# Where the first image's value rows are loaded and cast, and who copies the bias table: an attention and snake-MLP kernel on Trainium2

## The chip, the cores and the metric

The kernel runs on one NeuronCore of one Trainium2 chip. The metric is the device time of one execution in microseconds (us). The kernel before was timed in three runs: 383.49, 385.6 and 383.82 us, median 383.82. Its profile is of one more execution, of 383.39 us.

The engines of the core run independently and meet at semaphores: PE (matrix products), DVE (elementwise, reads PSUM), ACT (activation functions, reads PSUM), POOL (elementwise on SBUF, and the issuer of the software DMA queue q0, the only one here that casts while it copies) and SP (only issues DMAs, on the hardware queue q1). ACT can issue DMAs too (queue q10). Each engine does its own instructions strictly in the order in which the program emits them.

## The reference

```python
def _attn_ref(q, k, v, bias_table):            # (8, 8, 576, 64) each; table (32, 8)
    scores = scale * np.matmul(q, k.transpose(0, 1, 3, 2))
    ...                                        # bucket[i, j] depends on |i - j| only
    scores = scores + bias_table[bucket].transpose(2, 0, 1)[None]
    attn = np.exp(scores - np.max(scores, axis=-1, keepdims=True))
    attn = attn / (np.sum(attn, axis=-1, keepdims=True) + 1e-09)
    return np.matmul(attn, v)

def _moe_ref(x, w_in, w_out, alpha):           # x: (4608, 512), w_in (512, 2048)
    h = x @ w_in
    s = np.sin(alpha * h)
    return (h + s * s / (alpha + 1e-09)) @ w_out
```

There are 8 images of 8 heads. Each has 576 positions of 64 numbers. The bias of a pair of positions depends on their distance alone and is constant beyond 128 positions. The attention result of an image, heads side by side, is the input of the MLP.

## The kernel before, in words

**Per image t (0 to 7).** Heads are taken in pairs p = 0..3, and the pairs in groups g = 0, 1. A score unit is a pair of matmuls (two heads) into two PSUM banks: kind "A" is 128 keys by 512 queries for two heads, kind "C" the last 64 keys, kind "B" the last 64 queries (`plan_unit`, L638). ACT exponentiates a unit (L672) into the tile `u`. The bias enters afterwards as a product: DVE multiplies the band near the diagonal by exp(bias), tiles `m2r` and `mhr` (L696 and L681). The products with the values (`plan_av`, L830) take `v` and `vh` (values with a column of ones, so that the row sums come along); DVE normalizes (L864, L865), and the result is transposed into `xT` (on PE with a copy by ACT or DVE for image 0, by DMA later). In image 0 a group has ten units, eight "A" and two "C"; its "B" units are done later, among image 1 (`plan_late`).

**MLP per block b of 512 tokens.** `plan_moe_in` (L905): 16 tiles f of h = w_in^T x, 4 matmuls each; ACT sine (L929); a square by ACT or DVE; DVE forms g (L943). `plan_mo` (L975): 64 matmuls g^T w_out, used by the planner to fill PE while ACT exponentiates.

**The order.** A planner (class `Plan`, L60 to L196) decides at build time. Each task has a cost per engine, dependences, a priority and an earliest time `nb`; `run` simulates the engines and emits tasks in the order of that simulation. The constants `T_...` (L207 to L225) are such earliest times in us. They set only the order: on the chip an instruction starts when its engine has reached it and its semaphores allow it. A DMA issue also waits until the DMA issued eight places earlier on the same kind of queue (q0; SP and ACT together) has landed, since there are eight completion semaphores for each.

**The start, image 0.** Written out by hand from L480 to L533, then by the planner.

- k and q of pair 0 come in 32 bits on SP (L486, L487) and are cast by DVE, ACT and POOL (L519 to L523). Pairs 1 to 3 come by cast loads on POOL (`load_pair`, L492, L606). PE transposes each (`plan_tr`, L560: six transposes for pair 0, twelve for the others), and kT and qT are copied out of PSUM by DVE, or ACT for qT of pair 0 (`T_ACT`). POOL makes a block-diagonal copy of the last keys, `kt` (L598).
- The bias: ACT issues the loads of the table and of a constant `phi` (L488, L489), PE multiplies (L515), ACT exponentiates (`tabE`, L516), PE spreads it with `phi` (L518), DVE copies the result to `e_sb` (L520), ACT writes it to `e_dram` (L528), and SP reads it back in skewed windows as `m2r` and `mhr` (L529 to L532).
- The values: SP loads all of image 0 in 32 bits into a part of the tile of `w_out`: heads 0 to 3 and the last 64 rows early (L507 to L509), heads 4 to 7 behind the band rows (L533). POOL casts them to `v` and `vh` (L526, L419) in a fixed chain of nine tasks in `plan_v0`, and the products of group 0 and 1 depend on them (`vdone`, L856).
- alpha: SP loads `alphaN` and an identity `idf` (L510, L511), PE transposes (L626), DVE forms `alphaT` and `inv_a` (L629 to L633). The earliest time is 8.6 (`T_AL`).
- Image 1's values are loaded in 32 bits into `v1st` and cast by POOL (`loads3`, L540). POOL clears image 1's `kt`, `vh`, `v` (`clear`, L497) at the start. `load_w_in16` (L428), k and q of image 1 (`nat2`, L537) and `load_w_out16` (L434) follow on POOL, `w_in` in two halves.
- `warm` (L453) is matmuls on zeros.

Of the kernel before, what the change touches and what calls it, by code (L numbers as in the profile page):

```python
# [10 lines left out]
F16 = mybir.dt.float16  # L11
# [44 lines left out]
class Cell:  # L56
    v = None
# [150 lines left out]
T_WI = 15.0  # L208
T_FIRST = (4.9, 5.8)
T_PAIR = ((7.0, 7.4), (10.4, 11.0), (12.4, 13.0))  # L210
T_ACT = (0,)
T_M2 = (12.0, 13.5, 14.5, 14.5)
T_MH = 13.0
T_V0 = (8.0, 8.8, 9.6, 10.4, 11.0, 14.2, 14.8, 15.4, 16.0)
T_AL = (8.6, 100)
LATE = 100
T_LD = 27.0
# [4 lines left out]
T_V = (0.0, 50.0)  # L222
T_TR1 = (35.0, 36.5)
T_W = (22.5, 28.0)
T_WO = (40.0, 43.0, 46.0, 49.0)  # L225
WARM0 = 5
WARM1 = 1
# [20 lines left out]
def kernel(  # L248
# [45 lines left out]
    idf = nc.inline_tensor(np.eye(NF, dtype=np.float32), "identf")  # L294
# [15 lines left out]
    wv = w_out16.rearrange("p f n -> p (f n)")  # L310
    v1st = sgl.tile([128, 2 * (4 * H + NP) * D], F16, name="v1st")
    vst, vhst = [], []
    for x in (wv, v1st):
        n4 = 2 * 4 * H * D
        y = x[:, 0:n4].bitcast(F32)
        vst.append(y.rearrange("p (c h d) -> p c h d", c=4, h=H) if vst else
                   y.rearrange("p (y h c d) -> p y h c d", y=2, c=4, h=H // 2))
        vhst.append(
            x[:, n4 : n4 + 2 * NP * D].bitcast(F32).rearrange("p (hp d) -> p hp d", hp=NP)
        )  # L320
# [72 lines left out]
    def load_v16(t):  # L393
        vp = v[t].rearrange("h s d -> s h d")
        for c in range(4):
            nc.gpsimd.dma_start(  # L396
                out=vs[t % 2][:, c, :, 0:D], in_=vp[128 * c : 128 * c + 128],
            )
        vq = v[t].rearrange("(hp two) s d -> two s hp d", two=2)
        for z in range(2):  # L400
            nc.gpsimd.dma_start(
                out=vhs[t % 2][64 * z : 64 * z + 64, :, VC * z : VC * z + D], in_=vq[z, 512:S]
            )

    def load_v32(t, eng):
        vp = v[t].rearrange("h s d -> s h d")
        for c in range(4):
            eng.dma_start(out=vst[t][:, c], in_=vp[128 * c : 128 * c + 128])
        vq = v[t].rearrange("(hp two) s d -> two s hp d", two=2)
        for z in range(2):  # L410
            eng.dma_start(out=vhst[t][64 * z : 64 * z + 64], in_=vq[z, 512:S])

    def cast_v(t, eng, cs):
        for c in cs:
            if c < 4:
                eng.tensor_copy(out=vs[t][:, c, :, 0:D], in_=vst[t][:, c])
                continue
            z = c - 4
            eng.tensor_copy(  # L419
                out=vhs[t][64 * z : 64 * z + 64, :, VC * z : VC * z + D],  # L420
                in_=vhst[t][64 * z : 64 * z + 64],
            )
# [30 lines left out]
    def warm(n, k=7):  # L453
        for _ in range(n):
            full(pb[:, k, :], zz[:, 0:128], zz, True, True)
# [41 lines left out]
    clear(P_, 1)  # L497
    vp = v[0].rearrange("h s d -> s h d")
    vq = v[0].rearrange("(hp two) s d -> two s hp d", two=2)

    def v0_in(y, eng):
        for h in range(4):
            eng.dma_start(
                out=vst[0][:, y, h], in_=v[0, 4 * y + h, 0:512].rearrange("(c p) d -> p c d", p=128)
            )

    v0_in(0, nc.sync)  # L507
    for z in range(2):
        nc.sync.dma_start(out=vhst[0][64 * z : 64 * z + 64], in_=vq[z, 512:S])  # L509
    nc.sync.dma_start(out=alphaN, in_=moe_alpha.rearrange("(f p) -> f p", p=128))  # L510
    nc.sync.dma_start(out=idf_sb, in_=idf.ap())  # L511
# [5 lines left out]
    warm(WARM1)  # L517
    full(pb[0:H, 0, 0:EW], tabE, phi_sb, True, True)  # L518
    cast0(0, nc.vector)  # L519
    nc.vector.tensor_copy(out=e_sb, in_=pb[0:H, 0, 0:EW])  # L520
# [3 lines left out]

    def cast_v0(h):
        P_.tensor_copy(out=vs[0][:, :, h, 0:D], in_=vst[0][:, h // 4, h % 4])  # L526

    nc.scalar.dma_start(out=e_dram.ap(), in_=e_sb)  # L528
    load_m2r(nc.sync, 0, 2)  # L529
    load_mhr(nc.sync)  # L530
    load_m2r(nc.sync, 2, 4)
    load_m2r(nc.sync, 4, H)  # L532
    v0_in(1, nc.sync)  # L533
# [6 lines left out]
    def loads3():  # L540
        load_v32(1, P_)
        stage_kq(2)
        cast_v(1, P_, range(6))
# [59 lines left out]

    def plan_v0():
        for p in range(2, NP):
            plan.add({"POOL": 1.5}, lambda e, p=p: load_pair(p), [], -950 + 200 * (p - 2), nb=5.8)  # L606
        for i in range(9):
            vdone.append(plan.add(
                {"POOL": 0.7 if i == 4 else 0.4},
                lambda e, i=i: cast_v(0, P_, (4, 5)) if i == 4 else cast_v0(i if i < 4 else i - 1), [],  # L610
                9000 + i, nb=T_V0[i], after=vdone[-1:]))

        def rest(e):
            load_w_in16(1, (0, 2))
            loads2()

        x = plan.add({"POOL": 1.2}, lambda e: load_w_in16(0, (0, 2)), [], -400, nb=T_WI)
        x = plan.add({"POOL": 6.0}, rest, [], 9006, nb=T_WI + 3.0, after=vdone[-1:] + [x])
        plan.add({"POOL": 8.0}, lambda e: loads3(), [], 9007, nb=T_LD, after=[x])

# [462 lines left out]
```

## Time and profile before

| | before |
|---|---|
| three runs, median | 383.82 us (383.49 to 385.6) |
| the profiled execution | 383.39 us, of which the span of instructions is 381.6 |
| PE busy | 368.8 us (97%) |
| ACT busy | 313.9 us (82%) |
| DVE busy | 270.0 us (71%) |
| POOL busy | 92.5 us (24%) |
| share of the chain that ended last: PE, DMA | 86%, 8% |
| queue q0 (POOL): packets, MB | 90112, 18.06 |
| queue q1 (SP): packets, MB | 53520, 22.24 |
| first exponential of image 0 starts, last one ends | 9.26, 29.22 |
| first matmul on w_in, on w_out | 31.11, 48.86 |

A line of a timeline has the start, the duration, the engine, the line of the kernel, the operation, the tiles written and read, the count, and in brackets the idle time of the engine before it with what ended that. A line of the view by stretches has the stretch, and for PE, PE's weight loads, DVE, ACT and POOL the busy time and count, then the granted PE clock, the DMA engines' share and GB/s.

### The profile page before, as it was taken

The numbers are of one execution on the slowest core, as the hardware profiler recorded it, in microseconds if no ns is written. First come the engines' busy times: TensorE is split into PE (matmuls) and PEld (weight loads), VectorE is DVE, ScalarE is ACT, GpSimd is POOL, SyncE is SP. The second block draws the span as 40 slices with busy tenths as digits, with TensorE's granted clock in tenths as the row PEclk, the third lists the DMA queues.
The fourth block names the chain that finished last, engine by engine and source line by source line (L and its number), as shares of the span: only waits on it lengthen the run. The fifth ranks groups of instructions, "written<-read, shape, count | busy, mean of one in ns | idle before, by whom it ended". The sixth has DMA issues, their size and how long they took to land.

```text
span 381.6 us, 8918 instructions
## 1 busy us (share of the span) xinstructions
PE 368.8 (97%) x3545; PEld 200.5 (53%) x3545; DVE 270.0 (71%) x601; ACT 313.9 (82%) x432; POOL 92.5 (24%) x130
## 2 busy tenths in 40 slices
PE   6789999999999999999999999999999999999995
PEld 3355445644465446784564456544677456444442
DVE  4596997679676967697768867796769676999000
ACT  2798999879996999699988999699969997998111
POOL 7385371055000630046001900082005000000000
PEclk9999999999999999999999999999999999999999
DMA  9889999299713997279927991599239512000212
GB/s 179 163 153 206 198 214 161 60 165 123 81 48 86 159 132 90 78 137 115 137 52 155 94 161 51 112 117 155 56 92 141 59 53 78 3 0 3 82 55 82
DMA packets 143785, 40.90 MB, mean 107 GB/s; under 512 B 131624, under 2 KB 137824, under 8 KB 143744
## 3 DMA queue, kind: packets, MB, share of 16 engines
q0 software_dynamic: 90112, 18.06, 55.5%
q1 hardware_dynamic: 53520, 22.24, 24.3%
q8 instruction: 27, 0.44, 0.5%
q14 instruction: 14, 0.11, 0.1%
q10 hardware_dynamic: 112, 0.05, 0.1%
HBM read 37.73 MB, written 16.52 MB: 142 GB/s over the span
## 4 chain that ended last, share of the span: by engine, by line
PE 86%; DMA 8%; POOL 2%; ACT 2%; SPq 1%; DVE 0%; issue 0%; ACTq 0%; DVEq 0%
PE pb L451 85%; DMA nat<-in_q_dram 4%; DMA w_out<-in_v_dram 1%; DMA e_dram<-e_sb 1%; DMA xT<-xn 1%; DMA phi_sb<-phi_const 1%; POOL w_in L432 1%; PE pb L889 1%; ACT u L672 1%; PE pb L575 0%; POOL v L526 0%; SPq L467 0%; ACT kT L556 0%; SPq L474 0%; ACT s L929 0%
## 5 line engine op out<-in xcount | busy, mean ns | idle before, releaser
L672 ACT ACTIVATE u<-pb 128x1024 f16<-128x1024 f32 (+1 forms) x174 | 152.5, 963 | 11.4 <-PE pb L451 10.3
L451 PE MATMUL pb<-w_out,g 128*128 128x512 f16 x576 | 139.0, 380 | 0.1
L451 PE MATMUL pb<-xT,w_in 128*128 128x512 f16 (+4 forms) x704 | 128.0, 340 | 0.1
L929 ACT ACTIVATE s<-pb,alphaT 128x512 f16<-128x512 f32 x144 | 93.0, 687 | 14.8 <-PE pb L451 14.6
L943 DVE SCALAR_TENSOR_TENSOR g<-sq,inv_a,pb 128x512 f16<-128x512 f16 x144 | 101.1, 743 | 3.5 <-ACT sq L936 2.1
L451 PEld LDWEIGHTS <-w_in 128*128 128x128 f16 x704 | 64.1, 98 | 56.0 <-issue 0.6
L696 DVE TENSOR_TENSOR u<-u,m2r 128x512 f16<-128x512 f16 (+1 forms) x128 | 63.4, 504 | 30.8 <-ACT u L672 29.8
L451 PEld LDWEIGHTS <-g 128*128 128x128 f16 x576 | 52.9, 98 | 60.4 <-issue 8.5
L451 PEld LDWEIGHTS <-u 128*128 128x128 f16 x1404 | 53.6, 97 | 11.0 <-issue 3.8
L451 PE MATMUL pb<-v,u 128*128 128x65 f16 x1248 | 53.5, 193 | 0.0
L391 POOL COPY kt<-kT 64x256 f16<-64x256 f16 x12 | 5.4, 447 | 178.2 <-DMA kT<-staged_k 142.3
L451 PE MATMUL pb<-qT,kT 64*128 64x64 f16 (+1 forms) x512 | 43.6, 290 | 1.4 <-ACT u L672 0.9
L938 DVE TENSOR_TENSOR sq<-s 128x512 f16<-128x512 f16 x80 | 34.1, 431 | 10.9 <-ACT s L929 10.0
L936 ACT ACTIVATE sq<-s 128x512 f16<-128x512 f16 x64 | 40.4, 634 | 0.9
L451 PE MATMUL pb<-vh,u 128*128 128x130 f16 x156 | 34.4, 220 | 0.1
L865 DVE TENSOR_TENSOR xn<-pb,rd 128x256 f16<-128x256 f32 (+1 forms) x64 | 30.9, 482 | 2.4 <-DVE rd L864 0.2
L556 ACT ACTIVATE outs<-pb 128x512 f32<-128x512 f32 x15 | 9.0, 598 | 28.1 <-PE pb L451 28.1
L451 PEld LDWEIGHTS <-kT 64*128 64x128 f16 x512 | 16.8, 94 | 24.1 <-issue 16.4
L396 POOL DMA_DIRECT2D v<-in_v_dram x24 | 21.2, 898 | 0.1
L864 DVE RECIPROCAL rd<-pb 128x4 f32<-128x4 f32 (+1 forms) x64 | 11.9, 186 | 11.1 <-PE pb L451 10.0
L1004 ACT ACT_TABLE_LOAD x15 | 19.2, 1283 | 0.3
L558 DVE COPY outs<-pb 128x512 f32<-128x512 f32 x21 | 14.5, 689 | 4.0 <-PE pb L451 4.0
(80 smaller groups left out, 165.5 us busy)
## 6 DMA issues: line engine op xcount, KB each, us to landing
out_dram<-outs SPq DMA_DIRECT2D x36, 256.0 KB, 2.1
staged_k<-in_k_dram POOLq DMA_DIRECT2D x6, 576.0 KB, 8.2
staged_q<-in_q_dram POOLq DMA_DIRECT2D x6, 576.0 KB, 10.9
v<-in_v_dram POOLq DMA_DIRECT2D x24, 128.0 KB, 4.8
w_in<-in_moe_w_in_dram POOLq DMA_DIRECT2D x4, 512.0 KB, 7.6
w_out<-in_moe_w_out_dram POOLq DMA_DIRECT2D x4, 512.0 KB, 18.9
w_out<-in_v_dram SPq DMA_DIRECT2D x8, 128.0 KB, 6.2
v1st<-in_v_dram POOLq DMA_DIRECT2D x4, 256.0 KB, 18.1
```

The source lines that it names most:

```text
L396: nc.gpsimd.dma_start(out=vs[t % 2][:, c, :, 0:D], in_=vp[128 * c : 128 * c + 128],)
L451: nc.tensor.matmul(out=out, lhsT=lhsT, rhs=rhs, start=start, stop=stop)
L558: k_of(e).tensor_copy(out=o, in_=i)
L672: nc.scalar.activation(out=o, in_=x, func=AF.Exp, scale=0.125)
L696: nc.vector.tensor_tensor(out=io, in0=io, in1=m2[:, 2 * p : 2 * p + 2, x0 : x0 + hi - lo], op=ALU.mult)
L864: nc.vector.reciprocal(out=r, in_=x[:, :, :, D])
L865: nc.vector.tensor_tensor(out=xn.v[:, 0:nq].rearrange("p c (z d) -> p c z d", z=2), in0=x[:, :, :, 0:D], in1=r.unsqueeze(3).to_broadcast([ ...
L929: nc.scalar.activation(out=s16.v, in_=h.v, func=AF.Sin, scale=alphaT[:, f : f + 1])
L936: nc.scalar.activation(out=sq.v, in_=s16.v, func=AF.Square)
L938: k_of(e).tensor_tensor(out=sq.v, in0=s16.v, in1=s16.v, op=ALU.mult)
L943: nc.vector.scalar_tensor_tensor(out=gcell[b].v[:, f, :], in0=sq.v, scalar=inv_a[:, f : f + 1], in1=h.v, op0=ALU.mult, op1=ALU.add,)
L1004: nc.scalar.preload_act_table_set(name)
```

## The change

1. **Values of image 0.** Heads 0 to 3 and the last 64 rows are cast loads on POOL's queue (six DMAs, tasks of `plan_v0`); heads 4 to 7 still come in 32 bits on SP, behind the band rows, and four POOL copies cast them. The early loads of SP go. The products of group 0 no longer carry a planned dependence on `vdone`; they have the earliest times 17 and 19 (`T_V`).
2. **Bias table.** The copy to `e_sb` moves from DVE to ACT, and it and its matmul become planned tasks (`plan_table`); the matmul falls between the six k and the six q transposes of pair 0.
3. **Copies.** `T_ACT` is empty: DVE also copies qT of pair 0.
4. **alpha.** `alphaN` is loaded behind the values on SP; the identity is a POOL copy of a corner of `id_sb`; the earliest time of the transpose is 20. In the emitted order of PE it stands after the score matmuls of the sixteenth unit of image 0 (before: after those of the second).
5. **POOL's order.** Pairs 1 and 2 are loaded first, pair 3 behind the cast of q; `clear` of image 1 moves behind `w_in`; of `w_in`, half 0 stands before the four casts and half 1 after them and after the first two copies of L684; then L684's other two, `clear`, k and q of image 1, `w_out`. Image 1's values are cast loads (`load_v16`), without POOL casts.
6. **Warming.** Eight matmuls on zeros at the start in place of five and one later; three planned ones follow in place of one. Other earliest times move by up to a few us. In the emitted order of ACT, two copies to `xT` stand among image 0's exponentials in place of one. PE's order from image 1's first "B" units on is the same but for 3 `w_out` matmuls that come after those units in place of before.

The diff, cut:

```diff
-T_WI = 15.0
-T_FIRST = (4.9, 5.8)
-T_PAIR = ((7.0, 7.4), (10.4, 11.0), (12.4, 13.0))
-T_ACT = (0,)
-T_M2 = (12.0, 13.5, 14.5, 14.5)
-T_V0 = (8.0, 8.8, 9.6, 10.4, 11.0, 14.2, 14.8, 15.4, 16.0)
-T_AL = (8.6, 100)
+T_WI = 16.0
+T_E = 5.9
+T_CL = 26.0
+T_FIRST = (5.2, 6.3)
+T_PAIR = ((7.0, 7.4), (8.8, 9.4), (11.0, 11.6))
+T_ACT = ()
+T_M2 = (13.0, 14.5, 16.0, 16.0)
+T_RST = 27.0
+T_V0 = (7.5, 8.2, 8.9, 9.6, 10.3, 11.0)
+T_VB = 18.5
+T_AL = (20.0, 100)
...
-T_V = (0.0, 50.0)
+T_V = ((17.0, 19.0), (50.0, 50.0))
-WARM0 = 5
-WARM1 = 1
+WARM0 = 8
...
+    def load_vh(t, h):
+        nc.gpsimd.dma_start(
+            out=vs[t][:, :, h, 0:D], in_=v[t, h, 0:512].rearrange("(c p) d -> p c d", p=128)
+        )
+
+    def load_vt(t, z):
         vq = v[t].rearrange("(hp two) s d -> two s hp d", two=2)
+        nc.gpsimd.dma_start(
+            out=vhs[t % 2][64 * z : 64 * z + 64, :, VC * z : VC * z + D], in_=vq[z, 512:S]
+        )
...
     load_pair(1)
-    clear(P_, 1)
...
-    v0_in(0, nc.sync)
-    for z in range(2):
-        nc.sync.dma_start(out=vhst[0][64 * z : 64 * z + 64], in_=vq[z, 512:S])
-    nc.sync.dma_start(out=alphaN, in_=moe_alpha.rearrange("(f p) -> f p", p=128))
-    nc.sync.dma_start(out=idf_sb, in_=idf.ap())
+    load_pair(2)
+    P_.tensor_copy(out=idf_sb, in_=id_sb[0:NF, 0:NF])
...
     def loads3():
-        load_v32(1, P_)
+        load_v16(1)
         stage_kq(2)
-        cast_v(1, P_, range(6))
...
+    def plan_table():
+        b = Buf("h")
+
+        def mm(e):
+            full(bank(b)[0:H, 0:EW], tabE, phi_sb, True, True)
+
+        def cp(e):
+            nc.scalar.activation(out=e_sb, in_=bank(b)[0:H, 0:EW], func=AF.Copy)
+            nc.scalar.dma_start(out=e_dram.ap(), in_=e_sb)
+            load_m2r(nc.sync, 0, 2)
+            load_mhr(nc.sync)
+            load_m2r(nc.sync, 2, 4)
+            load_m2r(nc.sync, 4, H)
+            for h in range(4):
+                nc.sync.dma_start(
+                    out=vst[:, h], in_=v[0, 4 + h, 0:512].rearrange("(c p) d -> p c d", p=128)
+                )
+            nc.sync.dma_start(out=alphaN, in_=moe_alpha.rearrange("(f p) -> f p", p=128))
...
     def plan_v0():
...
+        plan.add({"POOL": 1.4}, lambda e: load_pair(3), [], -950, nb=5.8)
+        for i in range(6):
+            plan.add({"POOL": 0.7}, lambda e, i=i: load_vt(0, i - 2) if 2 <= i < 4 else
+                     load_vh(0, i if i < 2 else i - 2), [], 9000 + i, nb=T_V0[i])
+        for h in range(4):
+            vdone.append(plan.add({"POOL": 0.45}, lambda e, h=h: nc.gpsimd.tensor_copy(
+                out=vs[0][:, :, 4 + h, 0:D], in_=vst[:, h]), [], 9100 + h, nb=T_VB))
+        plan.add({"POOL": 2.5}, lambda e: clear(P_, 1), [], 9005, nb=T_CL)
+
+        x = plan.add({"POOL": 1.4}, lambda e: load_w_in16(0, (0, 2)), [], 9020, nb=T_WI)
+        for hf, nb in ((1, T_WI + 2.5),):
+            x = plan.add({"POOL": 1.4}, lambda e: load_w_in16(1, (0, 2)), [], 9021, nb=nb, after=[x] + vdone)
+        x = plan.add({"POOL": 6.0}, lambda e: loads2(), [], 9022, nb=T_RST, after=[x])
+        plan.add({"POOL": 8.0}, lambda e: loads3(), [], 9023, nb=T_LD, after=[x])
...
-            prev = [plan.add({"PE": 0.31}, mm, us + prev + ([] if t else vdone[0:5] if g == 0 else vdone), base + (AV_PRI if t else AV0) + i,
-                             nb=T_V[t] if t < 2 else 0.0, new=[ab] if i == 0 else [],
+            prev = [plan.add({"PE": 0.31}, mm, us + prev + (vdone if t == 0 and g else []),
+                             base + (AV_PRI if t else AV0) + i,
+                             nb=T_V[t][g] if t < 2 else 0.0, new=[ab] if i == 0 else [],
```

## The prediction

> **What bounds the kernel now.** First the page's busy times, then the busy time by stretches, because a share over the whole span hides stages with different limits.
>
> ```profile
> PE 368.8 (97%) x3545; PEld 200.5 (53%) x3545; DVE 270.0 (71%) x601; ACT 313.9 (82%) x432; POOL 92.5 (24%) x130
> ```
> ```profile
> 0.00:5.00 5.00, 2.31 (x5) 0.58 (x5) 1.94 (x9) 1.28 (x1) 3.96 (x15) 1.00 0.58 149
> 5.00:10.00 5.00, 4.37 (x44) 2.62 (x44) 2.15 (x4) 1.97 (x4) 3.81 (x9) 1.00 1.27 209
> 10.00:15.00 5.00, 2.73 (x18) 0.94 (x18) 1.32 (x4) 2.82 (x5) 2.41 (x7) 1.00 0.76 133
> 15.00:20.00 5.00, 4.56 (x62) 2.09 (x57) 4.42 (x11) 4.87 (x7) 0.83 (x2) 1.00 1.05 211
> 20.00:25.00 5.00, 3.88 (x68) 2.60 (x65) 4.94 (x12) 5.00 (x7) 4.23 (x9) 1.00 0.61 94
> 25.00:30.00 5.00, 4.32 (x81) 3.15 (x80) 4.83 (x17) 4.98 (x7) 5.00 (x7) 1.00 1.11 204
> 30.00:35.00 5.00, 5.00 (x54) 2.88 (x50) 2.03 (x7) 3.26 (x8) 2.55 (x7) 1.00 1.15 208
> ...
> 100.00:150.00 50.00, 50.00 (x512) 26.85 (x510) 37.41 (x86) 45.13 (x60) 10.22 (x11) 1.00 0.83 100
> ```
>
> The first number after the stretch's length is PE. From 30 us on PE is full (only 0.5 us of waiting, at 78.4, lies behind 50). PE's order there is almost unchanged. So the end moves by as much as the start of the dense part moves, if its DMAs come in time. Before 30, ACT is full from 13.5 (4.87, 5.00, 4.98 of 5) with DVE close behind; PE has holes. The stage to price is ACT's chain of image 0's twenty exponentials. Its timeline, and PE's at the hole:
>
> ```profile
> 9.26 2.19 ACT L672 ACTIVATE u<-pb 128x1024 f16<-128x1024 f32 x2 [0.76 <-PE pb L451]
> 13.49 13.62 ACT L672 ACTIVATE u<-pb 128x1024 f16<-128x1024 f32 x16 [2.04 <-PE pb L451]
> 26.87 0.52 ACT L556 ACTIVATE xT<-pb 128x256 f16<-128x256 f16 x1
> 27.14 2.08 ACT L672 ACTIVATE u<-pb 128x1024 f16<-128x1024 f32 x2
> 29.24 1.28 ACT L1004 ACT_TABLE_LOAD   x1
> ```
> ```profile
> 12.66 0.25 PE L626 MATMUL pb<-idf_sb,alphaN 16*128 16x16 f32 x1 [2.27 <-DMA idf_sb<-identf]
> ...
> 15.89 0.69 PE L575 MATMUL pb<-id_sb,nat 96*64 96x96 f16 x12
> ...
> 17.36 0.45 PE L575 MATMUL pb<-id_sb,nat 96*64 96x96 f16 x12
> ```
>
> PE stands 2.27 us on alpha's transpose, for an identity that SP loads behind six value loads. The score matmuls queued behind it are what ACT waits 2.04 us for. The chain of waits gives the other early steps:
>
> ```profile
> 7.30 4.53 DMA e_dram<-e_sb
> ...
> 15.34 5.71 DMA w_out<-in_v_dram
> ...
> 27.11 13.66 DMA nat<-in_q_dram
> ```
>
> **The parts, on ACT's chain.**
>
> (a) alpha's transpose leaves its place: -2.04. In its new place, behind the sixteenth unit, PE reaches it at about 21.5 (below), and `alphaN` must be there. SP issues it behind five band loads and four value loads. Those took from 11.91 to 18.87 to issue (14.79 + 4.08); without the 2.43 us outlier among the value issues (median 0.51) some 5 us. With `e_dram` at 10 to 11.8 the issue is at 15 to 17, and 5.6 to landing gives 20.6 to 22.6. Queued behind the wait would be a transpose to xT and the unit for which ACT comes at about 24. Cost 0 up to 22.6, and 1 us for each us later than 24; DVE's xT copy waits from 21.5. I take 0, range 0 to 0.7.
>
> (b) The first exponential. Before, `tabE` ended at 5.70, the `phi` matmul ran from 5.96 (0.58), then twelve transposes (1.14), a kT copy from 7.20 (0.74), pair 1's transposes, and score matmuls from 8.61 to the exponential at 9.26. Now six transposes come ahead of `phi`: 5.5 + 0.57, kT copied from 6.1 to 6.85, `phi` to 6.55, six more to 7.1, qT copied by DVE from 7.15 to 7.9 (0.75), score matmuls 0.61, exponential at about 8.6: -0.66. Bounds: 0 if q (landed 4.0 after its issue at 1.27) or pair 1 (PE waited for it until 7.74) decide as before, -1.2 if both come earlier since SP's 640 KB of values are no longer beside them. The e_sb copy (0.68 on DVE) falls on ACT between 6.5 and 7.2, where ACT idled 1.73 us before its qT copy: 0. If that cover goes, it is 0.7 on the first exponential. The qT copy of 0.65 leaves ACT.
>
> (c) One more xT copy among the exponentials. The one before moved the next exponential from 26.87 to 27.14: +0.27.
>
> (d) PE must now feed a chain without the hole. From the first unit's exponential on it issues 12 transposes, two units, 24 transposes and a "C" unit, while ACT has three exponentials of about 0.98 (13.62 us for twelve of these and four "C"), 2.9 us. With the rows up to 15.89 PE needs 0.65 + 1.1 + 1.3 + 0.66 = 3.7, with those from 17.36 on 0.45 + 0.78 + 0.9 + 0.42 = 2.55. So ACT idles between 0 and about 1.0 (0.8 here, some tenths at the later units). The rows up to 15.89 are the nearer ones, but the change packs PE denser: +0.4.
>
> [...]
>
> Sum: -2.04 - 0.66 + 0.27 + 0.4 = **-2.0**. The last exponential ends at about 27.2; behind it come a multiply, products, three normalizations and copies as before.
>
> **What lies beside it.** *DVE.* alpha's three operations (0.17 + 0.17 + 0.25) now fall among the multiplies. The first multiply ran at 16.14. The queue is emptier (GB/s 209 at 5 to 10 with the values in it), so I expect the band rows by 13 to 15, against 15 to 16 before. DVE's order from the first multiply to the last holds 16 "A" multiplies (8 x 0.41, 8 x 0.56), 4 x 0.25, 5 normalizations (0.63 each), two xT copies (0.28), one qT copy (0.75) and alpha (0.6): 13.8, less some 1.2 of overlapping starts, 12.6. From 14.6 it ends at 27.2, level with ACT. Each us that the rows come after 14.6 costs up to 1: 0, range -0.3 to +1.
>
> *POOL and q0.* Six cast loads are added (nearest rows: L396 0.90 to issue and 4.8 to landing for 1024 pieces of 256 B; L401 0.66): at most 4 x 0.9 + 2 x 0.66 = 4.9 us of POOL. Four casts (4 x 0.46) and the two of `vh` (0.86) go, and 2.3 us of `clear` moves from 2.9 to about 26. Heads 0 and 1 are issued at 8 to 10 and land by 15, before their products at about 18.7; head 3 stands behind the copies of `kt`, issued by 14, landed by 19, and is used at 20.5: hidden by the exponentials. If it were not, PE stands in order and each us counts. [...]
>
> *w_in, image 1's k and q, w_out.* Half 0 of w_in was issued at 21.6, now at about 16. The four casts wait for values issued behind the band rows: 13 to 16 plus 6.2 to landing is 19 to 22, and half 1 follows at about 23 (was 24.93). Then `clear`, and k and q of image 1 from 28.3 (was 26.32). They landed 11.6 and 13.7 us after issue since q0 works in order and half 1 was ahead, about 2.6 us per 512 KB (landings, by POOL's and PE's waits, 32.9, 35.3, 38.2, 40.8). Now half 1 is through at about 30, so q lands near 36, and PE wants it at 40.81 - 2 = 38.8 at most, 37.4 at least. Cost 0, with one us to spare. Later q0 items follow at the same pace, so w_out comes some 3 us sooner than before. The POOL casts of image 1's values at 54 to 59 go; PE is dense there: 0.
>
> **Rivals.** *The waits come back elsewhere* (0.28): bounds of (a), (b), (d) and DVE together, up to +0.7, +0.66, +0.6 and +1, of which I let half and more fall on the chain. The gain is 0.3 to 1.5, so 382.3 to 383.5. For it: DVE is at 4.83 and 4.94 of 5. Against it: no row shows the band rows late.
>
> *POOL holds back image 1's loads* (0.13), slower. In one queue now stand the four casts, which wait for SP's last values, half 1, two copies that wait for DVE's multiplies, `clear` and image 1's k and q. If the values land at 21 as before (15.34 + 5.71), nothing happens. At 22.5 the spare us is gone. From then on each us is a us on PE, which stands at k's and q's transposes, and the half of the values that waits is late for group 1's products too. At 24.5 it eats the gain; from about 26.4 the time is over 385.7, and at 27.5, six us later than before, it is 386.8. Against it: the queue that must be that late had 5.7 to 7.3 us to landing in every row.
>
> *The change does not do what it says*: the cast loads free SP, but `e_dram` (4.53 us for 8 KB) lands as late as before. That is the DVE bound above.
>
> **How the numbers follow.** -2.0 from 383.39 is 381.4; the median of the runs lies 0.43 above the profiled execution, so I forecast **381.8**. The forecast case has 0.59; its own range is 380.4 to 382.6, from the bounds of (b) and (d). A difference below 0.5%, 1.9 us, can't be told from no change here, so faster means below 381.9. Of the forecast case 0.45 lies there and 0.14 within; the first rival adds 0.28 within; the second 0.11 slower and 0.02 within: faster 0.45, same 0.44, slower 0.11. The range of 80% is 380.0 to 384.6: 0.12 left out above, 0.06 below.
>
> **What would show it.** Right: no idle of 2 us on ACT between 9 and 27; first exponential near 8.6; last ended at 27.2 +- 0.7; first w_in matmul near 29.1, first w_out matmul near 46.8; PE without waits from there. (a) is wrong if PE waits for `alphaN` by over 1 us; (d) if PE's transposes take 0.45 before 10 us (more gain); DVE if its first multiply comes after 15.5; POOL if PE waits for k or q of image 1 at 37. The whole is wrong if the start is 2 us earlier and the end is not: then something in the dense part bounds it that I do not see.

## The result, and the profile after

| | before | after |
|---|---|---|
| median of the runs | 384.32 us (383.49 to 386.41, 8 runs) | 387.49 us (386.67 to 388.62, 8 runs) |
| ratio to before, 95% interval | | 1.0078 [1.0052, 1.0104] |
| span of the profiled execution | 381.6 | 386.1 |
| first exponential, end of the last | 9.26, 29.22 | 8.58, 32.59 |
| first matmul on w_in, on w_out | 31.11, 48.86 | 34.38, 52.11 |

The change makes the kernel 0.8% slower; the forecast was 381.8. (Some executions below are disturbed, with a lower clock and a time some per cent longer: three of ten of e1, three of four of e3, which thus has no ratio, and one of twelve of p4; the medians leave them out, and the profiles of e1, e3 and p4, which are of such executions, serve for the order of events alone.)

The busy times of the page, then the view by stretches, with the columns explained above:

```profile
PE 371.7 (96%) x3549; PEld 201.9 (52%) x3549; DVE 270.0 (70%) x601; ACT 314.0 (81%) x432; POOL 89.9 (23%) x125
```
```profile
10.00:15.00 5.00, 5.00 (x60) 2.50 (x58) 2.96 (x6) 4.82 (x6) 3.64 (x8) 1.00 1.22 139
15.00:20.00 5.00, 4.86 (x59) 2.28 (x53) 4.36 (x13) 5.00 (x7) 1.54 (x4) 1.00 1.30 251
20.00:25.00 5.00, 1.44 (x24) 0.81 (x23) 1.95 (x6) 1.91 (x3) 1.34 (x3) 0.86 0.97 179
25.00:30.00 5.00, 3.27 (x27) 1.93 (x27) 1.94 (x9) 2.65 (x4) 2.36 (x6) 0.50 0.22 30
```

The old hole (10 to 15: PE 2.73 before, 5.00 now) is gone, and a bigger one stands at 21.4 to 26.7. The timelines of ACT and of PE, and two pieces of the chain of waits, say what it is:

```profile
8.58 3.11 ACT L649 ACTIVATE u<-pb 128x1024 f16<-128x1024 f32 x3 [1.46 <-PE pb L433]
11.87 10.04 ACT L649 ACTIVATE u<-pb 128x576 f16<-128x576 f32 x12 [0.18 <-PE pb L433]
27.35 0.38 ACT L511 ACTIVATE xT<-pb 128x256 f16<-128x256 f16 x1 [5.44 <-PE pb L868]
...
32.61 1.28 ACT L983 ACT_TABLE_LOAD   x1
```
```profile
26.73 0.26 PE L603 MATMUL pb<-idf_sb,alphaN 16*128 16x16 f32 x1 [5.29 <-DMA alphaN<-in_moe_alpha_dram]
...
34.38 0.81 PE L433 MATMUL pb<-xT,w_in 128*128 128x512 f16 x3
```
```profile
7.15 2.27 DMA e_dram<-e_sb
...
17.85 8.74 DMA alphaN<-in_moe_alpha_dram
```

PE stands 5.29 us on `alphaN`, whose DMA took 8.74 us instead of the 5.6 of before. PE's other work up to here is early or in time. POOL's timeline, with DMA issues in it:

```profile
15.10 1.39 POOL L414 DMA_DIRECT2D w_in<-in_moe_w_in_dram  x2
19.96 1.41 POOL L588 CAST v<-w_out 128x256 f16<-128x256 f32 x3 [3.46 <-DMA w_out<-in_v_dram]
26.49 0.41 POOL L588 CAST v<-w_out 128x256 f16<-128x256 f32 x1 [5.12 <-DMA w_out<-in_v_dram]
...
27.20 1.40 POOL L414 DMA_DIRECT2D w_in<-in_moe_w_in_dram  x2
...
34.06 0.80 POOL L408 DMA_DIRECT2D nat<-in_k_dram  x1
```

The last value head came as late as `alphaN`, so POOL stood 5.12 us, and w_in's second half and image 1's k and q (`nat`) went out late. They show little in PE's waits here (0.19 us on q at 43.10) because PE itself was 5.3 us late.

The rest of the loss of this execution is in the dense part, from the first matmul on w_out to the end: 386.1 - 52.11 = 333.99 against 381.6 - 48.86 = 332.74, +1.25. DVE, POOL and PE there:

```profile
53.67 3.38 DVE L553 COPY kt<-kT 64x64 f16<-64x64 f16 x2
```
```profile
52.62 2.21 POOL L372 DMA_DIRECT2D staged_k<-in_k_dram  x1 [2.51 <-DMA w_out<-in_moe_w_out_dram]
54.54 2.50 POOL L372 DMA_DIRECT2D staged_q<-in_q_dram  x1
```
```profile
57.88 0.39 PE L433 MATMUL pb<-w_out,g 128*128 128x512 f16 x1 [1.69 <-DVE g L922]
```

Two DVE copies of 0.18 us each last 3.38: the first ends at 54.84, the second at 57.05, and POOL's two issues of a large DMA end at 54.83 and 57.04. In the kernel before the same copies met only one such issue (1.32 us).

### The profile page after: what moved, and what is told of

It reads as the page before. It is cut to its first block, busy times and chain, and to the rows that moved or that the text cites. A ratio compares the mean times of both kernels' runs of the same rounds, so it can differ in the third digit from the quotient of the medians.

```text
span 386.1 us, 8917 instructions
## 1 busy us (share of the span) xinstructions
PE 371.7 (96%) x3549; PEld 201.9 (52%) x3549; DVE 270.0 (70%) x601; ACT 314.0 (81%) x432; POOL 89.9 (23%) x125
## 4 chain that ended last, share of the span: by engine, by line
PE 87%; DVE 4%; DMA 4%; SPq 2%; issue 1%; ACT 1%; ACTq 0%; DVEq 0%
PE pb L433 86%; DMA alphaN<-in_moe_alpha_dram 2%; DVE g L922 2%; SPq L574 1%; DMA phi_sb<-phi_const 1%; PE pb L868 1%; DVE kt L553 1%; DMA e_dram<-e_sb 1%; DVE sq L917 1%; ACT u L649 1%; SPq L449 0%; DVE xn L844 0%; SPq L456 0%; DVE u L674 0%; DVE qT L513 0%
## 5 line engine op out<-in xcount | busy, mean ns | idle before, releaser
L674 DVE TENSOR_TENSOR u<-u,m2r 128x512 f16<-128x512 f16 (+1 forms) x128 | 61.7, 490 | 32.7 <-ACT u L649 31.4
L389 POOL DMA_DIRECT2D v<-in_v_dram x28 | 24.8, 897 | 2.4 <-DMA nat<-in_q_dram 2.0
```

The costliest lines, as they stand in the source:

```text
L389: nc.gpsimd.dma_start(out=vs[t % 2][:, c, :, 0:D], in_=vp[128 * c : 128 * c + 128],)
L674: nc.vector.tensor_tensor(out=io, in0=io, in1=m2[:, 2 * p : 2 * p + 2, x0 : x0 + hi - lo], op=ALU.mult)
```

## The experiments

Theories, after this first look. **A**: the wait for `alphaN` is the loss. **B**: POOL, standing on the late value heads, holds image 1's loads back (the second rival). **C**: the value heads and `alphaN` are late because w_in's first half, issued at 15.1 instead of 21.6, shares the DMA engines with them. **D**: the held copies. **E**: the granted clock, 0.50 from 24 to 30, is a loss of its own. "Ratio" is to the kernel before on the same chip, with its 95% interval.

### The parts one by one: e1 to e4

**e1**, `alphaN` loaded early; **e2**, its transpose later; **e3**, w_in's first half behind the four casts; **e4**, DVE's copies with two inputs:

```diff
 e1      load_nat(nat0[:, 1], 0, 2, q[0], nc.sync)
+        nc.sync.dma_start(out=alphaN, in_=moe_alpha.rearrange("(f p) -> f p", p=128))
 e2
-T_AL = (20.0, 100)
+T_AL = (28.0, 100)
 e3
-        x = plan.add({"POOL": 1.4}, lambda e: load_w_in16(0, (0, 2)), [], 9020, nb=T_WI)
+        x = plan.add({"POOL": 1.4}, lambda e: load_w_in16(0, (0, 2)), [], 9020, nb=T_WI, after=vdone)
 e4 (load_kt on DVE)
-    tensor_copy(out=kts[t][r, p, r], in_=kTs[t][r, p, 512:S])
+    tensor_tensor(out=kts[t][r, p, r], in0=kTs[t][r, p, 512:S], in1=kTs[t][r, p, 512:S], op=ALU.max)
```

> The changed kernel, with the alpha vector's load issued on SP right behind pair 0's q instead of behind the four value loads. Theory A (the loss is PE standing 5.29 us on that load): the stall and with it 5.3 us go, about 382.2 us against 387.5. Theory B (the late value heads hold back POOL's queue as well): the fourth value head still lands near 26 us, w_in's second half and image 1's k and q follow late, and PE stands about 2 us at k's and q's transposes near 38 us: 384 to 385. If neither, 387.

> The changed kernel with one constant changed: the planned time of alpha's transpose is 28 instead of 20, so that PE meets it behind image 0's last products; every DMA is issued as before. Theory A: as in the run with the load first, about 382.2 us, and PE's first wait for alpha is under 0.5 us. Theory B: 384 to 385. If the place of the transpose does not matter, 387.

> The changed kernel with the first half of w_in issued on POOL behind the four casts instead of ahead of them. Theory C (what makes the value heads and alpha late is w_in's traffic beside them on the DMA engines): the value heads land by about 21 instead of 26.5, alpha by 23, PE's stall falls from 5.3 to under 1.5 us and the time to 383 to 384. Rival (SP's own queue is slow whatever POOL's does): the heads still land at 26, w_in's first half comes at 32 or later, and the time is 387 to 390.

> The changed kernel with DVE's copies of image 1's last keys written as a maximum of the tile with itself, the same values from an instruction with two inputs. Theory D (two of these copies, 1.1 and 2.2 us in place of 0.17, last until POOL has written its descriptors for the staging of image 2): they take 0.2 us each, PE's wait of 1.7 us near 57 us goes, and the time falls by 1.7 to 1.9, to about 385.7. Rival (they wait for something else, such as kT): no change, 387.5.

| | median, us | ratio |
|---|---|---|
| e1 | 386.16 (7 runs) | 1.0037 [1.0014, 1.0059] |
| e2 | 385.25 (10 runs) | 1.0028 [1.0001, 1.0055] |
| e3 | 386.77 (1 run) | none |
| e4 | 386.61 (10 runs) | 1.0035 [1.0018, 1.0052] |

A falls as the whole cause. By the medians e1 gives back 1.3 us of 5.3. e3's one run that counts shows no gain that can be told; in its profile the casts of the values start at 20.59 and PE does not wait for `alphaN`, as C has it. In e2 PE does not wait for `alphaN` at all, the first w_in matmul starts at 28.87, where the forecast had 29.1, and yet only 2.2 us come back (its profile is of one of the fastest of its ten runs, 383.38). PE's timeline of e2 has the next wait, image 1's k and q, the mechanism of B:

```profile
37.99 0.45 PE L530 MATMUL pb<-id_sb,nat 96*64 96x96 f16 x12 [0.70 <-DMA nat<-in_k_dram]
...
40.88 0.45 PE L530 MATMUL pb<-id_sb,nat 96*64 96x96 f16 x12 [1.47 <-DMA nat<-in_q_dram]
```

D is borne out in this: in e4 the copies beside the same POOL issue are short (DVE's timeline),

```profile
54.14 0.38 DVE L554 TENSOR_TENSOR kt<-kT 64x64 f16<-64x64 f16 x2
```

and the span from the first w_in matmul to the end falls from 351.7 to 349.8. What the hold costs depends on when the two meet: the two copies took 3.38 us in the changed kernel, 2.01 in e2 and 1.32 in the kernel before, and p0 below, without this edit, also has 349.6. What holds a copy of 0.18 us for up to 2.2 is not shown here, nor is what POOL does in that time: e4's and b3's texts say that it writes descriptors, and the traces have only its issues, instructions of 2.21 and 2.50 us.

### The old stall alone, and the parts together: b1, b3, e5, e7

b1 is the kernel *before* with e1's move of the loads of `alphaN` and the identity, b3 is b1 with e4's edit, e5 is e1 and e4 together, and e7 is e5 with POOL's order changed:

```diff
 e7, against e5
-T_KEEP, T_CL = 20.0, 26.0
+T_KEEP, T_CL = 24.0, 17.5
-        load_w_in16(1, (0, 2)) after the casts; then k and q of image 1, w_out
+        k and q of image 1 after the casts; then load_w_in16(1, (0, 2)); then w_out
```

> The kernel before with the loads of alphaN and of the identity moved on SP from behind the six value loads to right behind pair 0's q; nothing else. If step (a) priced the old stall rightly, the 2.04 us in which PE stood on alphaN go, all later work moves up by as much, and the time falls by 1.5 to 2.1 us (ratio 0.9945 to 0.9960); image 1's k and q, which PE awaited for only 0.21 us in the kernel before, then become late by up to 2 us and may take part of it back. Rival: the old stall was cover for a later wait, and the time stays within 0.5 us.

> The kernel before with the early alphaN and identity loads of b1, and with VectorE's two kt copies of image 1 written as an elementwise maximum of the tile with itself. If the copies are held while POOL writes descriptors (theory D), the 1.13 us of the held copy in the kernel before go as well as the alpha wait: time 3 us below the kernel before (ratio about 0.992). If the copy's length does not set PE's start, it equals b1.

> The changed kernel with two edits at once: alphaN right behind pair 0's q on SP, and kt copies as an elementwise maximum. If alphaN (5.3 us) and the held copies (1.9 us) were the whole loss, 387.5 less 7.2, about 380.3. If image 1's k and q are held on POOL behind the late value casts, PE stands 2 to 4 us at their transposes near 38 to 42 us of the span, and the time is 382.5 to 384.5. If a stall of this size there halves the granted clock behind it, some executions lie 2 us higher still.

> As e5, and POOL's order behind w_in's first half is changed: the clear of image 1's tiles comes ahead of the value casts, then image 1's k and q, then w_in's second half, then the keeps. If POOL's hold on image 1's k and q is what is left of the loss, they are issued about 5 us sooner, PE does not wait for them, first w_in matmul at 28.9 to 29.1, and the time is 380 to 381.5, below the kernel before by 3 to 4 us. If the transfers, and not the order on POOL, are what is late, it stays at e5's time; w_in's second half may take over as the wait near 31 to 33 us.

| | median, us (12 runs each) | ratio |
|---|---|---|
| b1 | 384.55 | 0.9989 [0.9968, 1.0009] |
| b3 | 384.19 | 0.9994 [0.9973, 1.0015] |
| e5 | 386.88 | 1.0046 [1.0016, 1.0075] |
| e7 | 385.19 | 1.0014 [0.9993, 1.0036] |

None of the four gains what the first branch of its text gives; b1 and b3 come out by the second. b1 shows that in the kernel before the 2.04 us stall was cover. With it gone, PE waits for DVE, and DVE for band rows that come no sooner (DVE's and PE's timelines of b1; its profile has its first w_in matmul only at 32.74, so the verdict rests on the twelve runs):

```profile
19.29 0.89 DVE L696 TENSOR_TENSOR u<-u,m2r 128x512 f16<-128x512 f16 x2 [1.62 <-DMA m2r<-e_dram]
...
20.74 0.75 DVE L558 COPY kT<-pb 128x576 f16<-128x576 f16 x1
```
```profile
21.55 0.29 PE L451 MATMUL pb<-vh,u 128*128 128x130 f16 x1 [2.24 <-DVE kT L558]
```

e5 has a like wait (2.2 us on DVE's qT copy), and e7 trades the wait on k and q for one on w_in (2.9) and on a cast (1.3). In e5, taking out 7 us of waits gives back 0.6 by the medians and 1.2 by the ratios: something paces the head that none of these touches.

### Bases, and the clock: p0, p1

From here on the kernels leave out the DMA transposes, which begin at 66 us (plain copies of the same bytes take their place, so that they compute other values there). The bases:

> The changed kernel with its DMA transposes (kT and qT of images 2 to 7, and part of xT from 66 us on) replaced by plain DMA copies of the same bytes, so it leaves out these transposes and computes from other values there; every instruction of the first 59 us is as it was. It is the base for the kernels with p in their names. Both theories: the head is the changed kernel's (first w_in matmul near 34.4, alphaN awaited 2 to 6 us), and the time within 2 us of 387.5.

> The kernel before with the same replacement of the DMA transposes from image 2 on (the transposes are left out); its head is untouched. Both theories: first w_in matmul near 31, time about 3 us below p0_after_plain, as the kernel before stands to the changed one.

387.63 us (1.0072 [1.0048, 1.0097]) and 384.25 (0.9983 [0.9961, 1.0005]): the bases stand as the originals do. p1 puts dummies into the wait:

```diff
             c.v = bank(b)
+            for _ in range(20):
+                full(c.v, zz[:, 0:128], zz, True, True)
             nc.tensor.transpose(out=c.v[:, 0:NF], in_=alphaN, identity=idf_sb)
```

> p0_after_plain (it leaves out the same transposes) with 20 matmuls of zeros (512 columns, 0.22 us each at full clock, 4.3 us) ahead of alphaN's transpose, written to that transpose's own bank. The wait for alphaN stays as long as it was, but PE is busy in it. If the granted clock of 0.50 from 24 to 30 us in the changed kernel is what an idle PE brings, that spell goes and with it 1 to 2 us against p0_after_plain. If the clock falls for another reason, or the half-clock work was hidden behind ACT's exponentials, the time stays within 0.5 us.

389.13 us (6 runs), 1.011 [1.0078, 1.0143]. PE is busy in every us from 22 to 31, and from 25 on the granted clock is 1.0 in its profile, where the changed kernel has 0.50, so there the fall came with the idle PE (p1's own spell, 0.50 from 22 to 24, stands behind a wait of 2.73 us on DVE); but nothing is gained. `alphaN` was issued at 22.71 there (the four value loads ahead of it on SP took 9.66 us to issue), and PE did not wait for it behind the dummies, which ran to 29.4, so that p1 does not price the spell. It gives no support to E for this place.

### VectorE's queue, or the stream of loads: p2 to p6

p2 is e5 on the base and with DVE's order changed; p3 is p2 with POOL's order of the kernel before; p4 and p5 move w_in's first half in p3; p6 is b3 on the base with DVE's order changed:

```diff
 p2
-T_M2, T_MH = (13.0, 14.5, 16.0, 16.0), 14.0
+T_M2, T_MH = (13.0, 17.5, 17.5, 17.5), 16.5
 p3, against p2: load_w_in16(0, ...) gets after=vdone
-T_KEEP, T_CL = 20.0, 26.0
+T_KEEP, T_CL = 30.0, 17.5
 p4, against p3: without after=vdone
-T_KEEP, T_WI, T_VB, T_RST = 30.0, 16.0, 18.5, 27.0
+T_KEEP, T_WI, T_VB, T_RST = 16.0, 19.0, 21.0, 26.0
 p5, against p3: without after=vdone
-T_KEEP, T_RST = 30.0, 27.0
+T_KEEP, T_RST = 24.0, 26.0
 p6, against b3
-T_M2, T_MH = (12.0, 13.5, 14.5, 14.5), 13.0
+T_M2, T_MH = (12.0, 17.0, 17.0, 17.0), 16.0
```

> p0_after_plain (the same transposes left out) with alphaN early, the kt copies as a maximum, and pair 3's qT copy ahead of pair 0's mhr product and pair 1's products on VectorE; POOL's order as in the changed kernel. If VectorE's queue behind the band rows gives back what alphaN saved, the 2.2 us wait for qT near 20 us is gone and the time is 1 to 2 us below e5's 386.9. If the holes in the loads take it back all the same (POOL idle on the value casts until 26, the DMA engines idle behind that), the wait moves to image 1's k and q near 38 to 42 us and the time stays at 386 to 387.

> p0_after_plain (the same transposes left out) with alphaN right behind pair 0's q on SP, the kt copies as a maximum, pair 3's qT copy on VectorE ahead of pair 0's mhr product and of pair 1's products, and POOL's queue in the order of the kernel before: w_in's first half behind the four value casts, the clear ahead of them, the keeps behind the loads of image 1 and of w_out. If the early w_in half is what makes the value heads late, and VectorE's queue behind the band rows what takes back the saved stall, all casts are done by 22.5 us, image 1's k and q are issued near 26, no wait over 1 us is left in the head, the granted clock stays at 1.0 there, and the time is 5 to 7 us below p0_after_plain and 2 to 4 us below p0_before_plain. If what is left lies elsewhere, it is no faster than p0_before_plain.

> p3_loads_in_old_order (the same transposes left out) with w_in's first half taken from behind the four value casts to ahead of them, and held back by the first two keeps and the clear, so that it is issued near 19.5 instead of 22.7. In p3 the DMA engines stand idle from 20.5 to 24.5 and run full from then to 50, and PE stands 2.4 us on w_in at 31.6 and 1.0 on image 1's q. If that hole in the stream of loads is what takes the saved time back, the hole closes, both waits go or fall below 0.5 us, and the time is 2.5 to 4 us below p3 (381 to 382.7), 1.5 to 3 below p0_before_plain. If the transfers as such (their bytes) are the limit, the value heads come late in its place, PE waits over 1 us for the casts of the values near 21 to 25, and the time stays within 1 us of p3's 385.2.

> p3_loads_in_old_order (the same transposes left out) with w_in's first half ahead of the clear and the casts, where the changed kernel has it (issued near 13.8 to 15), its second half and image 1's k and q still behind the casts. If w_in's half beside the band rows and the value heads is what makes them late, the casts end after 25 as in the changed kernel, PE stands 1 us or more on values or on VectorE's products between 18 and 26, and image 1's k and q are awaited for over 1 us: time 385 to 387, no better than p3. If only the hole counts, it is as fast as p4.

> p0_before_plain (the same transposes left out) with alphaN and the identity early, the kt copies as a maximum, and pair 3's kT and qT copies ahead of pair 0's mhr product and pair 1's products on VectorE; its loads stay in their order. If VectorE's queue alone took back the 2.0 us of the alphaN stall in the kernel before, the time falls 1.5 to 3 us below p0_before_plain's 384.25. If the loads (w_in, image 1's k and q) are next, they are awaited for 1 to 2 us more between 29 and 42 us, and the time stays within 0.7 us of 384.25.

| | median, us | ratio |
|---|---|---|
| p2 | 387.59 (6 runs) | 1.0073 [1.0051, 1.0095] |
| p3 | 385.22 (12) | 1.0021 [0.9998, 1.0045] |
| p4 | 383.03 (11) | 0.9948 [0.9922, 0.9974] |
| p5 | 384.75 (12) | 0.9994 [0.9975, 1.0014] |
| p6 | 384.98 (12) | 1.0012 [0.9986, 1.0038] |

p2 is the clearest run of the study. The wait for `alphaN` and the held copies are gone, 0.4 us of waiting on DVE's copies is left, the first w_in matmul is at 28.52, 5.9 us sooner than in the changed kernel, and the time is the changed kernel's. PE's longest waits, and the DMA engines by stretches (last columns: clock, share, GB/s):

```profile
PE pb L535 <- DMA nat<-in_k_dram: 3.7, 1, 3.7
PE pb L535 <- DMA nat<-in_q_dram: 2.1, 1, 2.1
```
```profile
22.00:24.00 2.00, 1.36 (x29) 1.03 (x26) 1.84 (x7) 2.00 (x4) 0.00 (x0) 1.00 1.10 201
24.00:26.00 2.00, 1.91 (x47) 1.57 (x45) 1.73 (x7) 1.69 (x4) 0.00 (x0) 1.00 0.30 59
26.00:28.00 2.00, 1.66 (x42) 1.43 (x40) 1.86 (x7) 1.98 (x3) 1.67 (x5) 1.00 0.01 4
28.00:30.00 2.00, 2.00 (x29) 1.27 (x27) 1.03 (x3) 1.30 (x4) 1.89 (x6) 1.00 0.59 72
30.00:32.00 2.00, 2.00 (x12) 0.94 (x11) 0.16 (x1) 1.26 (x3) 1.61 (x7) 1.00 1.11 209
...
34.00:36.00 2.00, 2.00 (x11) 0.93 (x10) 2.00 (x5) 2.00 (x5) 2.00 (x4) 1.00 1.08 149
36.00:38.00 2.00, 0.70 (x4) 0.10 (x1) 2.00 (x4) 2.00 (x5) 1.42 (x2) 1.00 1.13 161
```

From 30 us on the DMA engines are never idle until behind 45 (a share of 1.08 and more), and image 1's q lands in that stream, so the some 4 us in which next to nothing moves, because POOL's queue stands on the last value cast, are lost to k and q. They are not all of the 5.8 us, though. e2 has the same loads in the same order, issued at the same times to 0.2 us, and there PE takes q up at 40.88 against 43.17: p2's stream carries only 149 and 161 GB/s from 34 to 38, where e2's has 193 and 200, for a reason that no run shows. And behind these waits p2 has 10 us at a clock of 0.50, which take some 2.9 us more (see E below). p3 removes the late casts but not the hole (share 0.18 and 0.00 from 20 to 24), and there w_in is late, by 2.42 us at 31.56. p5 has the casts at 25.7 to 27.3, w_in being ahead of them, and PE waits 1.9 us on a cast and 1.3 on q: the lateness of C. In p4 w_in's half went out at 21.4 (the two keeps ahead of it took 1.89 us), so that the hole is only shortened, and it is the first to beat both kernels. p6 has the same limit in the kernel before: with DVE's queue freed, PE stands 2.94 us on k and q.

### The load order alone: p8, and with all else: p7

```diff
 p8, against p0_after_plain; p7, against p4, has the same five values but T_RST = 26.0
-T_KEEP, T_WI, T_CL, T_RST, T_VB = 20.0, 16.0, 26.0, 27.0, 18.5
+T_KEEP, T_WI, T_CL, T_RST, T_VB = 17.0, 18.0, 14.0, 24.0, 21.0
```

> p4_no_hole (the same transposes left out) with the clear moved into POOL's idle time near 15, so that w_in's first half is issued near 18.5 to 19.5 instead of 21.4, right behind the first two keeps. In p4 the DMA engines are still idle from 20 to 23, image 1's q lands near 41.4 and PE stands 0.7 and 2.4 us on image 1's k and q. If the date of these loads is set by the length of that hole, it is 1.5 to 3 us shorter here, q lands at 38.5 to 40, the two waits fall to under 1 us together, and the time is 1 to 2 us below p4's 383.2 (381.2 to 382.2), about 2.5 below p0_before_plain. If the value heads are pushed out by w_in again, PE stands on the casts near 21 to 25 and the time is p4's or worse.

> p0_after_plain (the same transposes left out) with p7's order of POOL's queue as the only edit: the clear and two keeps ahead of w_in's first half, which is issued near 18.5 to 20 instead of 14 to 15, then the casts, w_in's second half, image 1's k and q. AlphaN still stands behind the four value loads on SP, the kt copies and VectorE's order are the changed kernel's. If the early w_in half is what makes SP's loads late, the value heads and alphaN land by 23 (26 to 29 in the changed kernel), PE's wait for alphaN falls from 4 to 5.3 to under 2 us, and the time is 2 to 4 us below p0_after_plain's 387.6. If SP's queue is slow by itself, alphaN is awaited as long as before, and the time falls by less than 1 us.

p7: 381.35 us (7 runs), 0.9928 [0.9888, 0.9969]. p8: 383.27 us (12 runs), 0.9974 [0.9952, 0.9996]. Five constants turn the changed kernel (p0: 0.7% slower than before) into one that is some 0.3% faster, an interval that just clears 1. They move w_in's first half from 15.1 (the changed kernel, whose head p0 has) to 18.8, the clear and two copies of L684, the keeps, to ahead of it, and the other two keeps to other places; of the other engines' order up to the first w_in matmul only a group of nine products and a matmul on zeros, both on PE, change their place. POOL's timeline of p8, its stretches, and one row of its DMA issues (KB, median us to landing):

```profile
18.83 1.39 POOL L418 DMA_DIRECT2D w_in<-in_moe_w_in_dram  x2
20.22 1.43 POOL L592 CAST v<-w_out 128x256 f16<-128x256 f32 x3
...
23.89 1.40 POOL L418 DMA_DIRECT2D w_in<-in_moe_w_in_dram  x2
25.28 0.81 POOL L412 DMA_DIRECT2D nat<-in_k_dram  x1
```
```profile
20.00:22.00 2.00, 1.91 (x35) 1.18 (x31) 1.93 (x7) 2.00 (x3) 1.65 (x4) 1.00 0.95 116
22.00:24.00 2.00, 1.96 (x29) 1.37 (x27) 1.90 (x9) 1.59 (x4) 0.64 (x3) 1.00 1.13 212
24.00:26.00 2.00, 1.99 (x35) 1.40 (x34) 1.90 (x7) 2.00 (x3) 2.00 (x3) 1.00 1.13 210
26.00:28.00 2.00, 1.09 (x32) 0.97 (x29) 1.61 (x6) 1.98 (x4) 2.00 (x4) 1.00 1.05 187
```
```profile
alphaN<-in_moe_alpha_dram SPq DMA_DIRECT2D x1, 8.0 KB, 3.6
```

`alphaN` stands where it stood, behind the four value loads, and was issued at 17.35 (17.85 in the changed kernel, 19.07 in p0); it takes 3.6 us instead of 8.7 (8.6 in p0), and PE does not wait for it. The casts find their data (no idle bracket at 20.22), the hole is closed, and q is awaited for 0.64 us at 38.37. So C is shown as far as the date of w_in's first half decides the lateness, and with it the cause of A; how the DMA engines divide their time between the queues no run shows. Of B it is a part: k goes out at 25.28 instead of 34.06 in the changed kernel, but there the last keep, which waits 2.79 us for DVE, and 2 us of clear stood ahead of k as well, and p8 moves these too; what each is worth was not separated. With the DMA transposes in, this order was not run.

## Why the prediction was wrong

**(a), the step that failed.** "The issue is at 15 to 17, and 5.6 to landing gives 20.6 to 22.6", at a cost of 0. Both terms were too small. SP's timeline has the first:

```profile
9.43 0.41 SPq L449 DMA_DIRECT2D m2r<-e_dram  x1
...
12.44 5.37 SPq L574 DMA_DIRECT2D w_out<-in_v_dram  x4
17.85 1.30 SPq L577 DMA_DIRECT2D alphaN<-in_moe_alpha_dram  x1
```

The nine issues ahead of `alphaN` took 8.42 us, from 9.43 to 17.85, where I had "some 5", since I had left out an issue of 2.43 us as an outlier. It was none: with it the kernel before takes 6.96, and p8, with w_in out of the way, 7.32. `e_dram` landed at 9.42, before its range of 10 to 11.8, which hid most of this: 17.85 is 0.85 later than the latest bound. The landing then took 8.74, so 26.6, and this is the larger part. The 5.6 was a row from an execution in which no w_in lay beside it. I had moved w_in's first half to 16 in the same text and charged it nothing on SP's queue: with w_in issued ahead of it the landing is 8.1 to 8.7 (e2, p0, the changed kernel), with w_in issued 1.48 us behind it 3.6 (p8). The profile of the changed kernel gives the size: last exponential, first w_in matmul and first w_out matmul were forecast at 27.2, 29.1 and 46.8 and came at 32.59, 34.38 and 52.11, each later by 5.3 to 5.4, the wait for `alphaN`.

**The second rival** was the other half, with the same cause. "The queue that must be that late had 5.7 to 7.3 us to landing in every row", said the text against it; the last value head landed at 26.4 (its cast starts at 26.49), 11.5 us after its issue, where the rival's price reads "over 385.7". In the changed kernel its wait lies under that for `alphaN`; e2 and p2 uncover it.

**What was not priced**: the held copies, +1.25 in the dense part. 5.29 + 1.25 is the 6.5 us between the forecast span (379.6) and the measured one (386.1). This holds for these two executions: in the profiles of the pair p0 the dense part is no longer after than before (331.9 and 332.0), and 3.4 us are lost ahead of it.

**What held.** (b): first exponential at 8.58 for 8.6. So close a hit is in part luck: in other executions of the same start it lies between 7.76 (e4) and 9.08 (p0). A start faster than the bound of -1.2, 8.06, thus does occur. PE's transposes of pair 1, first in the changed kernel, then in e4:

```profile
7.02 0.69 PE L530 MATMUL pb<-id_sb,nat 96*64 96x96 f16 x12
6.46 0.45 PE L530 MATMUL pb<-id_sb,nat 96*64 96x96 f16 x12
```

The granted clock reads 1.00 at both places, and also in the kernel before where 0.69 falls to 0.45, so it does not show this difference; what decides it between executions stays open. (c) was one copy, as said. (d): ACT's idle time among the first fifteen exponentials is 0.18 for 0.4. `e_dram` took 2.27 us for 4.53 and DVE's first multiply came at 14.14, so the third rival is out. The cast loads of heads 0 to 3 were hidden. The gain on the way to the w_in matmuls is thus real: 28.5 to 28.9 in e2, p2 and p3 against 31.11. It shows in the time only where the loads keep pace, as in p8 (first w_out matmul 47.27, forecast 46.8).

**The -2.04 itself** was right for the changed kernel, whose band rows come sooner, and would have been wrong for an early `alphaN` alone: b1 gains nothing that can be told.

**E, the clock.** In ACT's stretch a spell at 0.50 costs nothing visible: with one from 24 to 30 the changed kernel is late by just its 5.29. Between the first w_in and the first w_out matmul it has a price. From the first w_in to the first w_out matmul take before 17.75 us with 0.21 of waiting on k and q; e2 20.02 with 2.17 and no spell, the waits alone but for 0.3; p6 22.06 with 2.94, p7 22.77 with 2.43 and p2 26.22 with 5.78, which leaves 1.6, 2.8 and 2.9 us over. These three have spells of some 3.4, 6.8 and 10.2 us there, the last in part while PE waits. PE's timeline of p7 has eight w_in matmuls in 3.59 us, where p8 has 1.90:

```profile
39.29 0.69 PE L535 MATMUL pb<-id_sb,nat 96*64 96x96 f16 x12 [2.43 <-DMA nat<-in_q_dram]
39.91 3.59 PE L437 MATMUL pb<-xT,w_in 128*128 128x512 f16 x8
```

So there a single stall of over 2 us costs, in these profiles, about half of the spell's working time more than its length. Waits of 2.27 us (the kernel before, up to 12.66), 2.24 (b1, up to 21.55) and 2.01 (p0, 19.29 to 21.30) brought no spell, one of 1.86 in e7 did, close behind another of 1.00; the length of one wait alone does not decide it.

**Open.** p7's seven runs lie in two groups, 380.5 to 381.4 (five) and 384.8 and 385.6 (two, with a lower mean clock, 0.987 for 0.996 and up); what decides between them within one program was not tried. The profile of p7 is of the slower group (384.75), that of p8 of its fastest run (381.87, clock 1.0, no spell), while most of p8's other runs have a mean clock of 0.985 to 0.995. Why `alphaN`'s 8 KB take 8.7 us beside w_in, and 3.6 in p8, is not shown: the runs moved w_in's issue in time and varied nothing else about it.

## What to carry to other kernels

A time to landing read from a trace holds for the loads that lay beside it in that trace (`alphaN`'s 8 KB: 5.6 us in the kernel before, 8.7 in the changed one, 3.6 in p8): when a change moves a large load, every load that now lies beside it has to be priced again, the small ones on other queues too. Here the loads kept the DMA engines busy without a break up to k and q (a share of 1.08 and more from 30 us on in p2), and a stall removed ahead of them paid only as far as that stream came sooner (387.59 us in p2, 383.27 in p8 with the hole closed); so look for stretches in which the DMA share falls, and for the queue that stands then. The large load did best here when the urgent small ones had just been issued: with w_in's first half at 15.1 `alphaN` took 8.7 us, with it at 22.7 (p3) the DMA share fell to 0.18 and 0.00 from 20 to 24, with it at 18.8 (p8) `alphaN` took 3.6 and the share stayed at 0.95 and more in each stretch of 2 us from 18 to 30.

## What was not expected of the hardware

- A DVE copy from SBUF to SBUF (64x64, 0.18 us) ended only when POOL's issue of a DMA of 4608 rows of 64 elements ended, after up to 2.2 us (the changed kernel); the same bytes by an operation with two inputs took 0.19 beside such an issue (e4).
- With w_in's first half (1 MB as stored in SBUF) issued on POOL's queue 2.75 us ahead of it, an 8 KB load on SP's queue took 8.7 us to landing (the changed kernel), with it issued 1.48 us behind 3.6 (p8). One of SP's value loads took 2.91 us to issue in the changed kernel; one took 2.43 in the kernel before, with no w_in in flight.
- The granted clock fell to 0.50 about 2.2 us after PE had gone idle and came back only some 4 us after it had work again (the changed kernel: idle from 21.4, work again at 26.73, 0.91 on average from 22 to 24, 0.50 from 24 to 30 and 0.88 from 30 to 32); in p0, by its stretches of half a us, these are about 2.6 and 5.4 us. Waits of 2.27 us (the kernel before), 2.24 (b1) and 2.01 (p0) did not bring it, one of 1.86 us close behind another of 1.00 (e7) did.
